# Gated mix of sliding-window attention and ReGLU with its gradients: the last stage in two passes, weight turns moved there, and more attention units turned in pairs by DMA

## The chip, the cores and the metric

The kernel runs on one core of one Trainium2 chip, in one launch. The metric is the device time in microseconds (us), as the median of several runs. Runs of one kernel agree within about 0.2%.

## What is computed

The reference computes an output and, by `jax.vjp`, the gradients of seven inputs. Cut to what matters (S = 2048 tokens, D = 512, F = 1376, 32 heads of 16, window 256, all bf16):

```python
def _A_ref(x, wqkv, wo):                      # sliding-window attention
    q, k, v = split_heads(x @ wqkv)           # 32 heads of 16
    scores = where(0 <= i - j < 256, q @ k.T * 16 ** -0.5, -1e9)
    return merge_heads(softmax(scores) @ v) @ wo

def _B_ref(x, W_gate, W_up, W_down):          # ReGLU
    gate = x @ W_gate
    h = relu(gate) * (x @ W_up)
    return h @ W_down

g = sigmoid((x * gate_w).sum(-1, keepdims=True))
out = g * _A_ref(x, wqkv, wo) + (1 - g) * _B_ref(x, W_gate, W_up, W_down)
# returned: out, and the gradients of x, wqkv, wo, W_gate, W_up, W_down, gate_w
```

## The kernel before

Tokens are handled in 16 tiles of 128. TensorE (PE) multiplies, VectorE (DVE) and ScalarE (ACT) evict and do elementwise work, GpSimd (POOL) masks and does small products, and the SyncE queue (SP) issues nearly all transfers in the order in which its program lists them.

**Stage 1, the feed-forward part** (to about 250 us). For 11 chunks of F and four groups of 512 tokens it computes h, the gradients of gate and up (`dgT`, `duT`), and the gradients of the three feed-forward weights. h, dgT and duT are written to DRAM, transposed to F x S (`hT_d`, `dgT_d`, `duT_d`).

**Stage 2, attention** (to about 721 us). Four head groups c of eight heads, and in each 16 block rows j of 128 queries. A block row meets up to three key blocks: the diagonal one (role "d"), the one before (role "m") and the far one (role "f"), each in two halves of four heads. One such piece is a *unit*: 90 a head group, 360 in all. A unit computes scores (`ST`, L683), their exponent on ACT (L693), a mask on POOL for roles d and f (L695, L698), the gradient of the probabilities (`dPT`, L707), its product on DVE (L712), and row sums (`BA`, L721 and L723). For the key-side gradients (`CD`, L541 and L544) the probabilities must be turned, in `flip`. There are two ways: by DMA, where both halves of a role go in one `dma_start_transpose` of 512 KB on the SP queue (a *pair*, `u.pair`, L740) or one half alone goes in 256 KB (`u.dma`); or on PE, in eight 128x128 transposes (`pt`, L750) and an eviction. Roles d always go in pairs and roles f always on PE. Roles m go in pairs in the first three head groups; in the last one:

```python
u.pair = u.role == "d" or (u.role == "m" and (c < DC - 1 or j in (3, 5, 7, 9)))
u.dma = u.pair or (u.role == "m" and half == 0 and (c < DC - 1 or j < 10))
```

The order of stage 2 is written by hand, unit by unit (`tc.manual_schedule()`): what is due after which unit stands in a queue of events, and background work is inserted by a running credit. The background work is the next group's projections (`project_parts`, L133 and L136), the previous head group's weight gradient (`grad_parts`, 16 pieces of four matmuls, `wps` at L637) and, from the dictionary `plan`, the loads of stage 3's weights. Those of Wqkv, Wg and Wu are turned by DMA out of DRAM, two 128-column chunks at a time (`turns`, L581). Their tiles reuse the slots of the transposed inputs (`x0` to `x3`, `d0` to `d3`) and of the projection weights (`p0` to `p3`) as these come free. `clear` (L584) zeroes on POOL the rows that the last, partial chunk of Wg or Wu leaves unused. At the end of a quarter of the block rows the key-side results are spilled to DRAM (`spill`, L564, into `dqkvo_d`).

**Stage 3, per token tile** (from about 721 us). For each of 16 tiles: `dwo` (4 matmuls, the output weight's gradient), `bps` (11, h x Wdown), `aps` (4, attention output x Wo), `dxps` (22 from dgT x Wg and duT x Wu, L1062, and 12 from the turned dqkv x Wqkv, L1066), then elementwise work and two stores. Loads come for groups of two tiles (`load_group`): h, dgT and duT (704 KB each), grad_out (`go_g`, 256 KB), the attention outputs (`o_g`, two of 128 KB), and a turn of 256 rows of `dqkvo_d` (1 MB, L845). For group 0 that turn is done early, in four parts, during stage 2 (`early_group`, L805), and h and dgT too (`early_f`). Stage 3 is not under the manual schedule. There the framework's scheduler orders each engine's instructions by its own costs, and may set an instruction that the program text has later between those of stage 2, where its buffers allow.

Of the kernel before, what the change touches and what calls it, by code (L numbers as in the profile page):

```python
# [9 lines left out]
ALU = mybir.AluOpType  # L10
# [12 lines left out]
def kernel(  # L23
# [490 lines left out]
    if True:  # L514
# [84 lines left out]
        def loads(name, src, k0, tag):  # L599
            def one(k):  # L600
                if (tag, "t") not in W6:
                    W6[(tag, "t")] = slot(tag)
                load_rows(name, src, k, W6[(tag, "t")][:, k - k0, :])
            return [lambda k=k: one(k) for k in range(k0, min(k0 + 4, FC))]
# [8 lines left out]
        def load_gw():  # L613
# [63 lines left out]
        def front(u):  # L677
# [6 lines left out]
            if not u.own:  # L684
                if u.half == 0:
                    kind = "m" if u.c == DC - 1 and u.j == 12 else u.role
                    tag = f"PP{kind}"
# [107 lines left out]
        def early_group():  # L795
            a = st.tile([P, NT, 4, P], BF, tag="rows_st", name="early")[:].rearrange("p t a n -> p (t a n)")
            n1 = 4 * DC * GT * P
            S2["T0"] = a[:, 0:n1].rearrange("p (c s) -> p c s", c=4 * DC)

            def grads():  # L800
                S2["grads"] = grad_parts(DC - 1, True)

            out = [grads]
            for k in range(4):
                out.append(lambda k=k: nc.sync.dma_start_transpose(out=S2["T0"][:, 4 * k:4 * (k + 1), :],  # L805
                                                                   in_=dqkvo_d[0:GT * P, k * D:(k + 1) * D]))
            return out

# [5 lines left out]
        def early_f(i):  # L814
            flat = wq.tile([P, 2, TPG, NP, P], BF, tag=f"z{i}", name=f"f{i}")[:].rearrange("p w k h q -> p (w k h q)")
            S2[f"f{i}"] = flat[:, 0:FC * GT * P].rearrange("p (c s) -> p c s", c=FC)
            load_f(S2[f"f{i}"], (hT_d, dgT_d)[i], slice(0, GT * P))

        def load_group(g):
            gsl = slice(g * GT * P, (g + 1) * GT * P)  # L820
            if g == 0:
                T_g, hT_g, dgT_g = S2["T0"], S2["f0"], S2["f1"]
                go_g = S2["g6"].tile([P, GT, D], BF, tag="go_g", bufs=1)
            else:
                flat = st.tile([P, NT, 4, P], BF, tag="rows_st", name="gt")[:].rearrange("p t a n -> p (t a n)")
                n1, n2 = 4 * DC * GT * P, (4 * DC + FC) * GT * P
                T_g = flat[:, 0:n1].rearrange("p (c s) -> p c s", c=4 * DC)
                hT_g = flat[:, n1:n2].rearrange("p (c s) -> p c s", c=FC)
                go_g = flat[:, n2:n2 + GT * D].rearrange("p (t d) -> p t d", t=GT)
                dgT_g = S2["g6"].tile([P, FC, GT * P], BF, tag="dgT_g")  # L830
                load_f(hT_g, hT_d, gsl)
            duT_g = S2["g6"].tile([P, FC, GT * P], BF, tag="duT_g")
            o_g = S2["g6"].tile([P, GT, DC, P], BF, tag="o_g")
            nc.sync.dma_start(go_g[:] if g == 0 else go_g, go_d[gsl, :].rearrange("(t p) d -> p t d", p=P))
            if g > 0:
                load_f(dgT_g, dgT_d, gsl)
            if g == 0:
                load_f(duT_g, duT_d, gsl)
            o_v = dqkvo_d[gsl, :].rearrange("(t p) (c a n) -> p t c a n", p=P, c=DC, a=4)
            for tl in range(GT):  # L840
                nc.sync.dma_start(o_g[:, tl, :, :], o_v[:, tl, :, 3, :])
            if g > 0:
                load_f(duT_g, duT_d, gsl)
            if g > 0:
                nc.sync.dma_start_transpose(out=T_g, in_=dqkvo_d[gsl, :])  # L845
            return hT_g, dgT_g, duT_g, T_g, go_g, o_g

        with tc.manual_schedule():
# [11 lines left out]
            early = []  # L860
# [25 lines left out]
            while n <= NU + LAG or ev or cdq or bgq:  # L886
                now = ev.pop(n, [])
                u = units[n] if n < NU else None
                if u is not None:
# [13 lines left out]
                    if u.first and u.j == TPG - 1 and u.c > 0:  # L903
                        bgq += ready
                    front(u)
                    if u.last and gi + 1 == len(groups) and u.j % TPG in (1, 3):
                        ev.setdefault(n + 2, []).append(("dma", lambda i=(u.j % TPG) // 2: early_f(i)))
# [65 lines left out]
                if u is not None and u.c == DC - 1 and not bgq and u.j > 6 and "T0" not in S2:  # L973
                    early = early_group()
# [4 lines left out]
                if early and calm and (u is None or n % 3 == 0 and u.j >= (9 if len(early) > 4 else 13)):  # L979
                    early.pop(0)()  # L980
# [10 lines left out]
            grp_next = load_group(0)  # L991
# [7 lines left out]
    with ExitStack() as p56:  # L999
        x_r5 = x_r  # L1000

        with ExitStack() as p6:
# [7 lines left out]
            dwo_ps = [ps6.tile([P, D], F32, name=f"dwo{c}") for c in range(DC)]  # L1010

            def add_dwo(t, tl, go_g, o_g):
                da_r = t6.tile([P, D], BF, tag="da_r", name="da_r")
                nc.vector.tensor_scalar(da_r[:], go_g[:, tl, :], g_all[:, t:t + 1], None, op0=ALU.mult)
                for c in range(DC):
                    nc.tensor.matmul(dwo_ps[c][:], lhsT=o_g[:, tl, c, :], rhs=da_r[:], start=t == 0, stop=t == NT - 1)
                if t == NT - 1:
                    for c in range(DC):
                        ws = t6.tile([P, D], BF, tag="ws", bufs=5, name="ws")
                        evac(ws[:], dwo_ps[c][:], ("act", "dve")[c % 2])  # L1020
                        nc.sync.dma_start(out_3[c * P:(c + 1) * P, :], ws[:])

            for g in range(NG):
                hT_g, dgT_g, duT_g, T_g, go_g, o_g = grp_next
                if g + 1 < NG:
                    grp_next = load_group(g + 1)
                for tl in range(GT):
# [3 lines left out]
                    if t > 0:  # L1031
                        add_dwo(t, tl, go_g, o_g)
                    bps = ps6r.tile([P, D], F32, tag="bps", bufs=1)
                    for fc in range(FC):
# [102 lines left out]
```

## Time and profile before

| | us |
|---|---|
| median of 3 runs (lowest, highest) | 909.26 (908.79, 910.39) |
| the profiled execution's own time | 911.05 |
| its span, first to last instruction | 909.4 |
| PE busy, share of the span | 895.0, 98% |
| DVE, ACT, POOL busy | 511.8, 441.3, 491.7 |
| SP's transfers (hardware queue 1), share of 16 DMA engines | 86.8% |
| granted TensorE clock | 1.000 |

Terms of the profile: L740 is line 740 of the kernel. "SPq" is the SP queue, whose bars are the issuing of transfers, not their way through the DMA engines. In the timeline a row has the start, the duration, the engine, the line, the operation and the tile written and read. In the chain of waits each row is a piece of the work that ended last, with its start and duration. A matmul's own bar is longer than the distance between matmuls, since they are pipelined; distances are used here.

### The profile page before, as it was taken

The page shows a single profiled execution, that of the slowest core. Times are in us where ns is not written, and L with a number is a line of the kernel's source. Part 1 is how long each engine was busy: PE and PEld are TensorE (multiplying, and loading weights), DVE is VectorE, ACT ScalarE, POOL GpSimd, SP SyncE. Part 2 cuts the span into 40 slices and gives each one's busy share as a digit, 9 for nine tenths or more (in the row PEclk, how much of TensorE's full clock was granted, in tenths as well). Part 3 has the DMA queues.
Part 4 walks back from the last instruction along what each step waited for, and adds up shares of the span by engine and source line. Part 5 has one row for each costly group of instructions (what it writes and reads, how often), then busy time and mean ns, then how long its engine had stood idle before and what let it go on. Part 6 is the DMA issues. An engine that isn't in the chain of part 4 may idle for free.

```text
span 909.4 us, 26127 instructions
## 1 busy us (share of the span) xinstructions
PE 895.0 (98%) x10711; PEld 566.7 (62%) x10711; DVE 511.8 (56%) x952; ACT 441.3 (49%) x778; POOL 491.7 (54%) x937
## 2 busy tenths in 40 slices
PE   9999999999989999999999999999999999999998
PEld 5555656655657777667776677766777644444445
DVE  4433334324468887678886788876787222333223
ACT  6422232222278777667776677766788211100001
POOL 4644545545267778767777567875677312222221
PEclk9999999999999999999999999999999999999999
DMA  9998879999799999999999989999999998777731
GB/s 301 203 194 186 197 179 207 211 207 216 180 143 158 180 188 194 184 175 156 177 185 187 180 161 182 187 182 184 184 185 186 235 269 227 186 181 185 182 86 46
DMA packets 505575, 169.06 MB, mean 186 GB/s; under 512 B 433456, under 2 KB 504336, under 8 KB 505456
## 3 DMA queue, kind: packets, MB, share of 16 engines
q1 hardware_dynamic: 484816, 145.51, 86.8%
q10 hardware_dynamic: 19008, 17.31, 7.2%
q0 software_dynamic: 1632, 4.59, 1.4%
q8 instruction: 83, 1.36, 0.6%
q14 instruction: 36, 0.29, 0.1%
HBM read 32.28 MB, written 36.24 MB: 75 GB/s over the span
## 4 chain that ended last, share of the span: by engine, by line
PE 80%; DMA 5%; DVE 4%; POOL 3%; issue 3%; SPq 2%; ACT 2%; ACTq 0%; POOLq 0%; DVEq 0%
PE dxps L1062 8%; PE ST L683 8%; PE dPT L707 7%; PE pt L750 6%; PE wps L412 5%; PE wps L637 5%; PE dxps L1066 4%; PE CD L541 4%; PE bps L1035 4%; PE BA L721 4%; PE pp L133 4%; PE dps L414 3%; PE ups L363 3%; PE gps L363 2%; PE CD L544 2%
## 5 line engine op out<-in xcount | busy, mean ns | idle before, releaser
L683 PE MATMUL ST<-z,K 128*128 128x512 bf16 x360 | 135.8, 378 | 2.6 <-DVE PPm L712 1.2
L707 PE MATMUL dPT<-z,V 128*128 128x512 bf16 x360 | 136.0, 378 | 1.9 <-DVE Pd L712 0.5
L695 POOL TENSOR_SCALAR_AFFINE_SELECT PPd<-PPd 128x512 bf16<-128x512 bf16 x126 | 80.0, 635 | 86.7 <-ACT PPd L693 86.7
L377 POOL TENSOR_TENSOR hT<-rg,upm 128x512 bf16<-128x512 bf16 x44 | 51.8, 1176 | 116.0 <-DVE upm L375 104.3
L412 PE MATMUL wps<-dgu_r,x_r 128*128 128x256 bf16 (+1 forms) x704 | 103.9, 270 | 1.8 <-DVE wst L74 1.8
L712 DVE TENSOR_TENSOR PPd<-PPd,dPT 128x512 bf16<-128x512 bf16 x126 | 85.4, 678 | 18.3 <-PE dPT L707 9.1
L698 POOL TENSOR_SCALAR_AFFINE_SELECT Pu<-Pu 128x512 bf16<-128x512 bf16 x112 | 71.9, 642 | 31.8 <-ACT Pu L693 30.7
L412 PEld LDWEIGHTS <-x_r 128*128 128x128 bf16 x704 | 68.4, 98 | 33.1 <-issue 2.6
L712 DVE TENSOR_TENSOR Pd<-Pu,dPT 128x512 bf16<-128x512 bf16 x112 | 76.3, 681 | 21.5 <-POOL Pu L698 10.6
L693 ACT ACTIVATE PPd<-ST 128x512 bf16<-128x512 f32 x126 | 76.1, 605 | 22.0 <-PE ST L683 19.7
L712 DVE TENSOR_TENSOR PPm<-PPm,dPT 128x512 bf16<-128x512 bf16 x122 | 81.4, 668 | 7.8 <-PE dPT L707 6.1
L693 ACT ACTIVATE Pu<-ST 128x512 bf16<-128x512 f32 x112 | 67.4, 602 | 34.1 <-PE ST L683 33.6
L693 ACT ACTIVATE PPm<-ST 128x512 bf16<-128x512 f32 x122 | 73.7, 604 | 20.2 <-PE ST L683 19.6
L1042 ACT COPY a_sb<-aps 128x512 f32<-128x512 f32 x16 | 9.4, 586 | 151.4 <-issue 137.7
L375 DVE SCALAR_TENSOR_TENSOR upm<-rg,ups 128x512 bf16<-128x512 bf16 x44 | 30.1, 685 | 82.9 <-ACT rg L369 40.3
L369 ACT ACTIVATE rg<-gps 128x512 bf16<-128x512 f32 x44 | 26.3, 598 | 91.8 <-PE gps L363 44.2
L72 ACT COPY p<-pt 128x1024 bf16<-128x1024 bf16 x67 | 68.5, 1022 | 3.8
L414 PE MATMUL dps<-db_r,h_r 128*128 128x512 bf16 x176 | 66.7, 379 | 0.0
L387 POOL TENSOR_TENSOR dgu<-dh_sb,rg 128x512 bf16<-128x512 bf16 x44 | 56.7, 1289 | 5.3 <-ACT dh_sb L383 5.3
L1048 POOL DMA_DIRECT2D out_dram<-o_sb x16 | 8.7, 542 | 88.8 <-DVE o_sb L1046 82.4
L637 PE MATMUL wps<-rows_st,x_r 128*128 128x384 bf16 x256 | 50.3, 325 | 0.0
L133 PE MATMUL pp<-x,p 128*128 128x512 bf16 x192 | 49.0, 378 | 0.0
(193 smaller groups left out, 2357.5 us busy)
## 6 DMA issues: line engine op xcount, KB each, us to landing
dqkvo_d<-rows_st SPq DMA_DIRECT2D x15, 512.0 KB, 4.0
hT_d<-hT ACTq DMA_DIRECT2D x44, 128.0 KB, 2.5
dgT_d<-dgu ACTq DMA_DIRECT2D x44, 128.0 KB, 3.0
duT_d<-dgu ACTq DMA_DIRECT2D x44, 128.0 KB, 2.9
duT_g<-duT_d SPq DMA_DIRECT2D x8, 640.0 KB, 5.2
gt<-hT_d SPq DMA_DIRECT2D x7, 640.0 KB, 5.8
dgT_g<-dgT_d SPq DMA_DIRECT2D x7, 640.0 KB, 5.0
out_dram<-wst SPq DMA_DIRECT2D x20, 128.0 KB, 2.7
```

What stands on the lines that cost most here:

```text
L72: nc.scalar.copy(out, in_)
L133: nc.tensor.matmul(pp[:], lhsT=w_p[c][:, cd, which * P:(which + 1) * P], rhs=x_T[tg][:, cd, :], start=(cd == 0), stop=(cd == DC - 1))
L412: nc.tensor.matmul(acc["w"][:, c, 0:2 * nw], lhsT=x_r[:, t, c * P:(c + 1) * P], rhs=k.dgu_r[:, :, i, s0:P], start=(go_ and c % 2 == 0), st ...
L414: nc.tensor.matmul(acc["d"][:], lhsT=k.h_r[:, i, :], rhs=db_r[:, t, :], start=go_, stop=no_)
L637: nc.tensor.matmul(wps[:], lhsT=x_r[:, t, part * P:(part + 1) * P], rhs=sts[c][:, t, 0:3, :], start=first and t == t0, stop=last and t == ...
L683: nc.tensor.matmul(ST[:], lhsT=KTt[:, ksl], rhs=z[:, 0, :, jl, :], start=True, stop=True)
L693: nc.scalar.activation(u.Pu[:], ST[:], ACT.Exp)
L695: nc.gpsimd.affine_select(out=u.Pu[:], in_=u.Pu[:], compare_op=ALU.is_ge, fill=0.0, base=0, pattern=[[0, HH], [1, P]], channel_multiplier=-1)
L698: nc.gpsimd.affine_select(out=u.Pu[:], in_=u.Pu[:], compare_op=ALU.is_ge, fill=0.0, base=-1, pattern=[[0, HH], [-1, P]], channel_multiplier=1)
L707: nc.tensor.matmul(u.dPT[:], lhsT=VTt[:, ksl], rhs=z[:, 1, :, jl, :], start=True, stop=True)
L712: nc.vector.tensor_tensor(out=u.Pd[:], in0=u.Pu[:], in1=u.dPT[:], op=ALU.mult)
L1062: nc.tensor.matmul(to, lhsT=src[:, fc, lsl], rhs=W6[(wt, fc)][:, cols], start=(fc == 0 and wt == "Wg"), stop=False)
```

## The change

1. Stage 3 becomes two passes over the tiles. Pass one has `bps` and `dwo`; the product with Wdown is copied by ACT into a buffer `b_all` in SBUF. Pass two has `aps` and `dxps` and reads `b_all`. The loads split in two: `load_a` (h, grad_out, attention outputs) and `load_b` (turned dqkvo, dgT, duT, grad_out again). `load_b` turns 1 MB for every group; the early turn in four parts is gone.
2. The turns of Wu and of the last chunks of Wg leave `plan` for a list `W_rest`, taken from in pass one, two items a group. Wdown is loaded in three whole transfers and a rest in place of eleven.
3. In the last head group role m goes in pairs for all block rows but the last two; single halves by DMA are gone.
4. The third head group's gradient pieces are released in four portions (at block rows 3, 6, 10, 12) in place of one.

The core of the diff:

```diff
         plan = {2: [load_gw], 5: turns("wqkv", A_wqkv, 0, 4, "p0"), 7: turns("wqkv", A_wqkv, 4, 8, "p1"),
                 11: turns("wqkv", A_wqkv, 8, 12, "p2"),
                 12: turns("Wg", B_W_gate, 0, 4, "x0") + turns("Wg", B_W_gate, 4, 8, "d0"),
-                13: turns("Wg", B_W_gate, 8, 12, "x1") + turns("Wu", B_W_up, 0, 4, "d1") + [lambda: clear("Wg")],
-                14: turns("Wu", B_W_up, 4, 8, "x2") + turns("Wu", B_W_up, 8, 12, "d2"),
-                15: loads("Wd", B_W_down, 0, "x3") + [lambda: clear("Wu")] + loads("Wd", B_W_down, 4, "d3") + loads("Wd", B_W_down, 8, "p3") + [load_wo]}
+                15: loads("Wd", B_W_down, 0, "x3") + loads("Wd", B_W_down, 4, "d3") + loads("Wd", B_W_down, 8, "p3")}
+        W_rest = (turns("Wg", B_W_gate, 8, 12, "x1") + [lambda: clear("Wg")] + turns("Wu", B_W_up, 0, 4, "d1") + turns("Wu", B_W_up, 4, 8, "x2")
+                  + turns("Wu", B_W_up, 8, 12, "d2") + [lambda: clear("Wu")])
...
-                        u.pair = u.role == "d" or (u.role == "m" and (c < DC - 1 or j in (3, 5, 7, 9)))
+                        u.pair = u.role == "d" or (u.role == "m" and (c < DC - 1 or j < NT - 2))
                         u.own = u.role == "f"
-                        u.dma = u.pair or (u.role == "m" and half == 0 and (c < DC - 1 or j < 10))
+                        u.dma = u.pair
...
+        def load_a(g):
+            if g > 1:
+                load_h(g)
+            S2[f"go{g}"] = load_go(g)
+            o_v = dqkvo_d[tokens(g), :].rearrange("(t p) (c a n) -> p t c a n", p=P, c=DC, a=4)
             for tl in range(GT):
...
+                o_t = pjA.tile([P, DC, P], BF, tag=("K0", "K1", "V0", "V1")[t % 4], name="o_t")
+                nc.sync.dma_start(o_t[:], o_v[:, tl, :, 3, :])
+                S2[f"o{t}"] = o_t
+
+        def load_b(g):
+            if g % 2 == 0:
+                S2["T"] = st.tile([P, NT, 4, P], BF, tag="rows_st", name="turned")[:].rearrange("p t a n -> p (t a n)")
+            n1 = 4 * DC * GT * P
+            T_g = S2["T"][:, g % 2 * n1:(g % 2 + 1) * n1].rearrange("p (c s) -> p c s", c=4 * DC)
+            nc.sync.dma_start_transpose(out=T_g, in_=dqkvo_d[tokens(g), :])
...
-                    if u.first and u.j == TPG - 1 and u.c > 0:
-                        bgq += ready
+                    if u.first and u.c > 0 and u.j in ((3, 6, 10, 12) if u.c == DC - 1 else (3,)):
+                        k = NT // 4 if u.c == DC - 1 else NT
+                        bgq += ready[:k]
+                        del ready[:k]
...
-            grp_next = load_group(0)
+            while late:
+                late.pop(0)()
+            load_a(0)
+            for _ in range(2):
+                W_rest.pop(0)()
+            load_a(1)
...
+            for t in range(NT):
+                g, tl = t // GT, t % GT
+                if tl == 0:
+                    if 0 < g < NG - 1:
+                        load_a(g + 1)
+                    for _ in range(2):
+                        if W_rest:
+                            W_rest.pop(0)()
+                    if g == NG - 2:
+                        load_wo()
+                    if g == NG - 1:
+                        grp_next = load_b(0)
...
+                nc.vector.tensor_scalar(da_r[:], S2[f"go{g}"][:, tl, :], g_all[:, t:t + 1], None, op0=ALU.mult)
+                bps = ps6r.tile([P, D], F32, tag=f"r{t % 3}", name="bps")
+                for fc in range(FC):
+                    nc.tensor.matmul(bps[:], lhsT=S2[f"h{g}"][:, fc, lsl], rhs=W6[("Wd", fc)],
+                                     start=(fc == 0), stop=(fc == FC - 1))
+                nc.scalar.copy(b_all[:, t, :], bps[:])
                 for c in range(DC):
...
+                    nc.tensor.matmul(dwo_ps[c][:], lhsT=S2[f"o{t}"][:, c, :], rhs=da_r[:], start=t == 0, stop=t == NT - 1)
```

In the order in which the built programs' instructions stand on each engine, stage 2 before has 104 more PE transposes than after. On SP, after, the six turns of Wu and the first two whole turns of `dqkvo_d` stand among the last head group's pairs; the two turns of Wg's end stand behind its last pair. On POOL, after, the zeroing of Wu's last rows stands before the mask of unit d of block row 4 (second half) of the last head group.

More of the change, by code (lines that the diff above doesn't have):

```diff
@@ L599, in loads, with whole @@
         def loads(name, src, k0, tag):
[L600 to L604, printed above, removed]
+            k1 = min(k0 + 4, nfull)
+            def whole():
+                W6[(tag, "t")] = slot(tag)
+                for k in range(k0, k1):
+                    W6[(name, k)] = W6[(tag, "t")][:, k - k0, :]
+                nc.sync.dma_start(W6[(tag, "t")][:, 0:k1 - k0, :], src[k0 * P:k1 * P, :].rearrange("(c p) d -> p c d", p=P))
+            return [whole] + [lambda k=k: load_rows(name, src, k, W6[(tag, "t")][:, k - k0, :]) for k in range(k1, min(k0 + 4, FC))]
         def load_wo():
@@ L793 @@
         NG = NT // GT
[L795 to L807, printed above, removed]
         def load_f(dst, src_d, gsl):
@@ L1009 @@
             pending_dgw = None
-            dwo_ps = [ps6.tile([P, D], F32, name=f"dwo{c}") for c in range(DC)]
-            def add_dwo(t, tl, go_g, o_g):
-                da_r = t6.tile([P, D], BF, tag="da_r", name="da_r")
-                nc.vector.tensor_scalar(da_r[:], go_g[:, tl, :], g_all[:, t:t + 1], None, op0=ALU.mult)
-                for c in range(DC):
[L1016 to L1021, printed above, removed]
+            dwo_ps = [ps6.tile([P, D], F32, tag=f"w{c}", name=f"dwo{c}") for c in range(DC)]
@@ L1030 @@
                     lsl = slice(tl * P, (tl + 1) * P)
[L1031 to L1034, printed above, removed]
-                        nc.tensor.matmul(bps[:], lhsT=hT_g[:, fc, lsl], rhs=W6[("Wd", fc)],
-                                         start=(fc == 0), stop=(fc == FC - 1))
-                    aps = ps6r.tile([P, D], F32, tag="aps", bufs=1)
+                    aps = ps6r.tile([P, D], F32, tag=f"r{t % 2}", name="aps")
                     for c in range(DC):
```

81 lines of the change are left out of this document (33 added, 48 removed).

## The prediction

> **What bounds the kernel now.** I read the page first (slices, chain of waits), then the chain in order of time for the last 300 us, the timelines of SP, PE and POOL through the attention stage, groups by tile, and the order in which both programs' instructions stand on each engine. The page's chain by engine:
>
> ```profile
> PE 80%; DMA 5%; DVE 4%; POOL 3%; issue 3%; SPq 2%; ACT 2%; ACTq 0%; POOLq 0%; DVEq 0%
> ```
>
> PE holds the end nearly everywhere. In the last stage the chain in order of time is the same five rows for each of 16 token tiles, without a gap:
>
> ```profile
> 744.01 0.86 PE dwo L1016 x4
> 744.87 2.37 PE bps L1035 x11
> 747.25 0.86 PE aps L1039 x4
> 748.11 4.75 PE dxps L1062 x22
> 752.94 2.61 PE dxps L1066 x12
> ```
>
> 2.37/11 is 0.216 us a matmul; a tile has 53, 11.5 us. Next the SP queue, where a bar begins when the instruction's waits are over. First a stretch of the third head group, which the change leaves alone:
>
> ```profile
> 540.76 1.96 SPq L740 DMA_TRANSPOSE p2m<-PPm  x1
> 542.83 3.81 SPq L740 DMA_TRANSPOSE p2d<-PPd  x1
> ...
> 557.17 3.28 SPq L740 DMA_TRANSPOSE p2m<-PPm  x1
> 560.61 2.77 SPq L740 DMA_TRANSPOSE p2d<-PPd  x1
> ```
>
> Eight turned pairs (512 KB each) stand end to end here in 22.6 us: 2.8 us each, or 185 GB/s. In the last head group SP goes on like this without a pause. I added its bars from 591.7 (after the spill at 591.0) to the end of the last pair,
>
> ```profile
> 703.69 6.14 SPq L740 DMA_TRANSPOSE p2d<-PPd  x2
> ```
>
> that is 709.8: 20 pairs 61.6 us (3.08 each), 5 half pairs 6.2, 14 weight turns 20.9 (1.49), 3 turns of rows 4.6, 4 "early" turns 5.2, 19 plain transfers 12.6 (0.66): 111 of 118.1 us. The queue is as full as PE. Only slack keeps it off the chain: the last pair landed near 712.5 (5.6 us after issue is the median) and PE reads it 5.2 us later:
>
> ```profile
> 717.73 0.18 PE L541 MATMUL CD<-rq,p2d 128*128 128x32 bf16 x1
> ...
> 718.14 2.90 PE L637 MATMUL wps<-rows_st,x_r 128*128 128x384 bf16 x16
> 720.87 0.81 PE L1035 MATMUL bps<-x,f 128*128 128x512 bf16 x3
> ```
>
> **The change part by part: PE.** The two passes run 15 and 38 matmuls a tile, 53 as before: 0. Thirteen units are no longer turned on PE (the second halves of block rows 1, 2, 4, 6, 8; both halves of 10 to 13). The chain shows such a unit as 0.46 us for its 8 transposes: 13 x 0.46 = -6.0 us, all on the chain. Their evictions (1.02 us on ACT or 0.69 on DVE) go too, but stand beside PE: 0. The third group's gradient pieces (0.65 us each) only spread out. The kernel's tail keeps its matmuls; PE has no gap over 0.1 us before its last half tile (900.8), so freeing the buffer there brings 0 to -0.3; I take 0.
>
> The Trainium skill's TensorE: Matmul & The Clock Gate, Part 4: PE-mode transpose, gives about 275 ns for one transpose inside a kernel; by that the 104 would save an estimated 28.6 us. The trace does not agree: they follow each other at 0.46/8 = 58 ns.
>
> **SP in the last head group.** The built order tells what the diff doesn't: the turns of Wu stand outside the hand-written schedule, and the scheduler puts all six of them back into the attention stage, with two whole 1 MB turns of dqkvo for the second pass; only the two of Wg's end stay behind. From the same spill to the last pair SP now has 29 pairs, 12 weight turns, 3 rows, 2 whole turns, 17 plain transfers. At 2.8, 1.49, 1.55, 5.8 and 0.66 us, with 1.9 for gaps: 81.2 + 17.9 + 4.6 + 11.6 + 11.2 + 1.9 = 128.4 us, against 118.1. (A whole turn lies between 5.2, four early ones at 1.31, and 6.3, the median of its own row in the last stage; I take the middle, as the queue has few other loads there.) That is +10.3, less the slack of 5.2: +5.1 at the stage's end. With pairs at 3.08, this stretch's own mean, +13; at 2.6, -1, which PE's own pace replaces at -6.0.
>
> **A new wait on POOL.** The zeroing of Wu's last rows (L584, 0.5 us) waits for the turn that fills them, and stands on POOL just before the select of the diagonal unit of block row 4, second half. Everything later queues behind it: the selects, so DVE's products, so PE's row sums. That select ran here:
>
> ```profile
> 618.62 0.64 POOL L695 TENSOR_SCALAR_AFFINE_SELECT PPd<-PPd 128x512 bf16<-128x512 bf16 x1 [1.81 <-ACT PPd L693]
> ```
>
> After the change POOL gets there about 3.5 us sooner (two turned units, 0.9, and four gradient pieces put off, 2.6): 615.1. SP reaches the end of that weight turn after 7 pairs, 8 weight turns, one of rows and two plain transfers: 591.7 + 19.6 + 11.9 + 1.55 + 1.3 = 626.1; its issue began at 624.6, and such turns land thus:
>
> ```profile
> DMA to landing us min/median/max: 3.6/5.0/6.1
> ```
>
> 629.6, and the memset ends at 630.1: POOL is 15.0 us late. PE works about two units (2.5 us) ahead of a select, so 12.5 us come off it. -6.0 + 12.5 = +6.5. Ends: pairs at their shortest bar (1.77) and the quickest landing leave about 6, pairs at 3.08 with the slowest 18.
>
> The two delays run beside each other: while POOL waits, SP works off its queue, so the later one decides, plus some idling of SP when PE then feeds it late. I take +9 (ends -6 and +16). To stay at zero cost the turn would have to land by about 617.6, 12 us before my estimate.
>
> **Pass one.** It has 15 x 0.216 = 3.24 us a tile, 6.5 us for a group's h (704 KB), go and o (256 KB each), on two h buffers: h of group g+1 may be issued only when group g-1 is through. From the stage's start T: SP's list puts a whole turn (6.3 us, the loaded median) straight before h of group 5. It follows an o that waits for tile 6 (T+22.7), so h is issued at about T+29.7 instead of T+25, lands 6.2 later (5.8 median and its first issue) at T+35.9, and is wanted at T+32.4: 3.5 late. The same before group 7: 2.7. Bytes: six h, ten go, 16 o, four dgT or duT, two whole turns and small ones, 4.2 + 2.6 + 2.0 + 2.8 + 2.1 + 0.8 = 14.5 MB in 57 us (with 5 us of head start), 254 GB/s, while the stage's best 10 us windows moved 281 to 286, so there is little to catch up with. I take +5; 0 if the turns are quick and h needs only its issue and 5 us, 10 if the early groups slip too. The 52 us of tiles hide the rest.
>
> **Pass two** has 38 matmuls, 16.6 us a group, for 2.7 MB of loads and 9 us of SP time: 0, as the last stage before carried 3.65 MB in 23 us. The whole turns come two groups ahead.
>
> **Sum.** +9 + 5 = +14 us on the profiled span of 909.4, so 923.4; the time around the span (911.05 - 909.4 = 1.65) stays. The profiled run is 1.8 above the median of the three, 909.26, so the median goes to 923.
>
> **The rivals.**
> - *Cheap turns* (faster). If a pair holds SP only for its shortest bar, 1.77 us, SP's total is 98 us and never binds; if in addition the weight turn lands before POOL gets there, all of PE's 6.0 us stay and pass one is fed: 909.3 - 6.0 = 903.5. It decides when that turn lands by 617.6. For: single bars of 1.8 to 2.1 exist. Against: each is followed by one of 2.8 to 3.8, the sum of two is 5.2 to 6.1. Chance 0.10.
>  The Trainium skill's DMA: Bandwidth & Descriptors, Latency and other measured facts, has a DMA transpose at 261 GB/s; by that a pair would be an estimated 2.0 us and the queue would not bind. The trace gives 185 GB/s end to end.
> - *Only the POOL wait or only pass one costs something*, the other is hidden: -6 + 6 to 12.5, or 0 + 5: 909 to 915. For: SP's slack of 5.2 and 6 us of head start for pass one. Chance 0.23, a fifth of it within 0.2%.
> - *The forecast*: the full last head group and a few late h: 915 to 935. Chance 0.57.
> - *Pass one bound by transfers throughout*: its 14.5 MB at the mean 186 GB/s of the page take 78 us instead of 57, +21 in place of +5: 939. For: the turns from DRAM are slow. Against: 281 and 286 GB/s in windows of this stage. Chance 0.10.
>
> That the change doesn't do what it says is in the forecast already: were the Wu turns really moved, SP would have 8.9 us less and POOL no wait, which leads to the first rival.
>
> **How the numbers follow.** The likeliest case gives 923. The range is 907 to 937: it leaves out most of the first rival and the last one. 0.2% is 1.8 us, about what a measurement of this kernel tells from none. Faster 0.12 (the first rival and a bit of the second), same 0.05, slower 0.83.
>
> **What would show it.** In the profile after: 104 fewer transposes on the line that turns units on PE, SP without a pause from 592 to past 720; POOL idle for 10 us or more at L584 near 615 to 630, PE idle beside it; the first bps near 730 instead of 720.87; gaps in PE before tiles 10 and 14 of pass one. The prediction is wrong if PE has no gap near 620 and the first bps starts before 718, or if pass two, which I hold for gapless, stalls.

## The result, and the profile after

The changed kernel takes 935.33 us (median of 6 runs, 933.81 to 938.13), the kernel before 910.32 in the same comparison (6 runs, 908.79 to 910.55): ratio 1.028, 95% interval 1.0265 to 1.0300. The forecast was 923, its range 907 to 937: the time lies inside the range, but the loss, 25.0 us, is nearly twice the forecast's 13.7 (923 against 909.26). The profiled execution has a span of 934.8 us, 25.4 more than before, and it takes 1.8 us more than its span.

Stages by the first ST of the last head group, the first `bps` and the first `aps` in the trace:

| | before | after | difference |
|---|---|---|---|
| up to the last head group (same work) | 585.0 | 582.9 | -2.1 |
| last head group to first `bps` | 135.9 | 148.9 | +13.0 |
| pass one (before: 15 of 53 matmuls a tile, 51.7) | 51.7 | 66.6 | +14.9 |
| the rest | 136.8 | 136.4 | -0.4 |

The first row is no effect of the change: over all traces of this study the last head group begins between 582.5 and 585.9. So stages are compared by their lengths. From the page of the changed kernel, PE and granted clock in 40 slices of 23.4 us, and the chain by engine:

```profile
PE   8999999999999999999999999969997888999998
...
PEclk9999999999999999999999999988999989999999
...
PE 65%; issue 11%; POOL 8%; DMA 6%; SPq 3%; DVE 3%; ACT 3%; POOLq 0%; ACTq 0%; DVEq 0%
```

Two places show, slice 27 (the last head group) and slices 31 to 34 (its end and pass one), and the clock beside them (27, 28 and 33); before, PE and clock were at 9 in all of these. The chain's larger shares of POOL and "issue" come mostly from stage 1, where it now runs through POOL's products; that stage is no longer than before.

**The last head group.** POOL's timeline (the bracket is the idle time before the row and what ended it):

```profile
617.80 0.40 POOL L781 TENSOR_TENSOR rows_st<-BAs,rinv 128x128 bf16<-128x128 f32 x1
629.17 0.51 POOL L584 MEMSET d<- 32x512 bf16 x1 [10.97 <-DMA d<-in_B_W_up_dram]
629.65 0.62 POOL L701 TENSOR_SCALAR_AFFINE_SELECT Pu<-Pu 128x512 bf16<-128x512 bf16 x1
```

This is the wait that the forecast named, and it ended where the forecast put it (629.7, forecast 630.1). PE has a hole of 8.6 us beside it (622.4 to 631.0). Stretches of 2 us; columns: length, PE busy (instructions), granted clock, DMA share, GB/s:

```profile
622.00:624.00 2.00, 0.45 (x8) 1.00 1.26 124
624.00:626.00 2.00, 0.00 (x0) 0.98 1.01 295
626.00:628.00 2.00, 0.00 (x0) 0.50 0.89 169
...
634.00:636.00 2.00, 2.00 (x14) 0.50 1.23 256
636.00:638.00 2.00, 2.00 (x32) 0.96 0.72 120
```

The clock falls to half 3.5 us after PE stops and stays there for 5 us after PE has begun again. Yet this hole is not what the stage pays for, as the runs below show. SP went on through it, and at the stage's end it still had this to do:

```profile
692.28 2.27 SPq L743 DMA_TRANSPOSE p2d<-PPd  x1
694.64 5.36 SPq L832 DMA_TRANSPOSE turned<-dqkvo_d  x1
...
703.60 1.85 SPq L743 DMA_TRANSPOSE p2d<-PPd  x1
705.50 5.90 SPq L832 DMA_TRANSPOSE turned<-dqkvo_d  x1
...
717.88 7.63 SPq L743 DMA_TRANSPOSE p2d<-PPd  x2
```

The last pair ends at 725.5 (before 709.8). Two whole turns stand between pairs, and PE waits for the pairs behind them: before `CD` and `ST` it has gaps of 1.0, 2.4, 1.4 and 1.6 us from 698 on. The first `bps` follows 6.3 us after the last pair, where it was 11.0.

**Pass one.** PE at the first and longest gap, and what SP did before it issued that h:

```profile
744.87 1.03 PE L1029 MATMUL dwo<-da_r,o_t 128*128 128x512 bf16 x4
752.24 1.89 PE L1025 MATMUL bps<-x,h 128*128 128x512 bf16 x4 [6.35 <-DMA h<-hT_d]
```

```profile
730.46 4.05 SPq L581 DMA_TRANSPOSE x<-in_B_W_gate_dram  x2
...
737.18 4.98 SPq L633 DMA_DIRECT2D out_dram<-ws  x4
...
743.87 0.43 SPq L799 DMA_DIRECT2D duT_g<-duT_d  x1
...
746.03 0.38 SPq L799 DMA_DIRECT2D h<-hT_d  x1
```

h of group 2 goes into the buffer that tile 1 gave up at about 739. It is issued at 746, behind two weight turns, four stores of gradients and the first loads of pass two, and PE waits for it. Gaps of 2.3 and 1.3 us follow before tiles 10 and 14, and 0.8 us before the first `dwo`: 10.8 us in all. The first four `bps` matmuls after the long gap take 1.89 us, elsewhere 1.03: the clock is at half again. Tile 4's eleven take 4.05 instead of 2.37, tile 10's about 1.5 us too many: 3.2 us more. Gaps and clock make 14.0 of the 14.9 us.

**Pass two** has no gap over 0.25 us. The chain in order of time, start and duration:

```profile
831.72 0.86 PE aps L1045 x4
832.59 4.75 PE dxps L1068 x22
837.41 2.61 PE dxps L1072 x12
```

### The profile page after: what moved, and what is told of

Read it like the earlier page. It is cut to its first block, busy times and chain, and to the rows that moved or that the text cites. A ratio compares the mean times of both kernels' runs of the same rounds, so it can differ in the third digit from the quotient of the medians.

```text
span 934.8 us, 25877 instructions
## 1 busy us (share of the span) xinstructions
PE 890.2 (95%) x10506; PEld 562.0 (60%) x10607; DVE 508.0 (54%) x946; ACT 445.2 (48%) x787; POOL 497.1 (53%) x937
## 4 chain that ended last, share of the span: by engine, by line
PE 65%; issue 11%; POOL 8%; DMA 6%; SPq 3%; DVE 3%; ACT 3%; POOLq 0%; ACTq 0%; DVEq 0%
PE dxps L1068 8%; PE ST L687 8%; PE dPT L710 7%; PE pt L753 5%; PE wps L641 5%; PE dxps L1072 4%; POOL dgu L387 4%; PE CD L541 4%; PE BA L724 4%; PE pp L133 4%; PE bps L1025 3%; PE CD L544 3%; POOL hT L377 2%; PE BA L726 2%; DMA h<-hT_d 2%
## 5 line engine op out<-in xcount | busy, mean ns | idle before, releaser
L687 PE MATMUL ST<-z,K 128*128 128x512 bf16 x360 | 136.5, 380 | 14.4 <-DVE Pd L715 8.6
L710 PE MATMUL dPT<-z,V 128*128 128x512 bf16 x360 | 136.4, 379 | 1.3 <-ACT PPd L696 0.5
L715 DVE TENSOR_TENSOR PPd<-PPd,dPT 128x512 bf16<-128x512 bf16 x128 | 86.9, 679 | 21.4 <-PE dPT L710 12.1
L1057 POOL TENSOR_TENSOR amb<-amb,go_g 128x512 f32<-128x512 f32 x16 | 24.6, 1540 | 73.8 <-DMA out_dram<-ws 62.9
L72 ACT COPY p<-pt 128x1024 bf16<-128x1024 bf16 x59 | 60.1, 1019 | 4.6 <-PE pt L753 0.5
L414 PE MATMUL dps<-db_r,h_r 128*128 128x512 bf16 x159 | 60.3, 379 | 0.0
L1079 POOL DMA_DIRECT2D out_dram<-dx_sb x15 | 8.1, 541 | 74.4 <-DVE dx_sb L1077 64.5
```

The costliest lines, as they stand in the source:

```text
L414: nc.tensor.matmul(acc["d"][:], lhsT=k.h_r[:, i, :], rhs=db_r[:, t, :], start=go_, stop=no_)
L687: nc.tensor.matmul(ST[:], lhsT=KTt[:, ksl], rhs=z[:, 0, :, jl, :], start=True, stop=True)
L710: nc.tensor.matmul(u.dPT[:], lhsT=VTt[:, ksl], rhs=z[:, 1, :, jl, :], start=True, stop=True)
L715: nc.vector.tensor_tensor(out=u.Pd[:], in0=u.Pu[:], in1=u.dPT[:], op=ALU.mult)
```

## The experiments

Lengths of stages are taken from each run's trace as in the table above ("attention" is the last head group to the first `bps`). The ratio is to the kernel before, with its 95% interval. The trace is of one execution: for e7 (916.4 us) and e10 (915.4) it is the longest of eight (910.2 to 916.4) and of ten (911.7 to 915.4), 4.1 and 2.3 us above the median, so their stage lengths are less typical than the others'.

| run | attention | pass one | median us | ratio |
|---|---|---|---|---|
| the change | 148.9 | 66.6 | 935.3 | 1.028 (1.0265 to 1.0300) |
| e1_clear_late | 148.1 | 64.0 | 933.1 | 1.0255 (1.0237 to 1.0273) |
| e2_pass_one_in_order | 138.0 | 53.5 | 915.6 | 1.0060 (1.0045 to 1.0075) |
| e3_pairs_as_before | 142.6 | 58.9 | 923.3 | 1.0146 (1.0127 to 1.0165) |
| e4_turns_in_the_plan | 151.4 | 58.2 | 931.5 | 1.0238 (1.0221 to 1.0255) |
| e5_pairs_alone | 144.4 | - | 918.6 | 1.0099 (1.0084 to 1.0114) |
| e6_passes_alone | 140.6 | 57.7 | 920.6 | 1.0115 (1.0098 to 1.0133) |
| e7_order_by_hand | 133.8 | 59.6 | 912.3 | 1.0030 (1.0014 to 1.0045) |
| e8_order_by_hand_wg | 129.4 | 64.1 | 916.6 | 1.0080 (1.0063 to 1.0097) |
| e9_h_on_act | 148.0 | 62.7 | 932.3 | 1.0241 (1.0210 to 1.0271) |
| e10_by_hand_h_on_act | 133.0 | 57.5 | 913.1 | 1.0030 (1.0017 to 1.0042) |
| e11_by_hand_wg_h_on_act | 129.5 | 59.3 | 910.6 | 1.0007 (0.9995 to 1.0020) |
| e12_fewer_bytes | 146.5 | 65.5 | 934.4 | 1.0270 (1.0257 to 1.0283) |
| e13_by_hand_late_turn | 129.4 | 51.8 | 907.2 | 0.9969 (0.9956 to 0.9982) |
| e14_by_hand_wg_back | 133.3 | 51.8 | 909.0 | 0.9990 (0.9980 to 0.9999) |
| e15_by_hand_wo_early | 130.6 | 52.6 | 905.3 | 0.9947 (0.9934 to 0.9959) |
| e16_by_hand_h_on_sp | 129.4 | 56.5 | 909.3 | 0.9988 (0.9977 to 0.9998) |
| e17_by_hand_units_on_pe | 134.9 | 51.9 | 910.1 | 0.9998 (0.9988 to 1.0007) |

### POOL's wait or SP's queue

The zeroing of Wu's rows held back:

```diff
-                  + turns("Wu", B_W_up, 8, 12, "d2") + [lambda: clear("Wu")])
+                  + turns("Wu", B_W_up, 8, 12, "d2") + [lambda: clear_late("Wu")])   # writes b - b of tile 5
```

> The change, with one edit: the zeroing of Wu's last rows is made to need the result of token tile 5 of pass one (it writes b - b there), so it can no longer stand in POOL's queue in the last head group; the turns stay where they are. In the changed kernel POOL idles 10.97 us before that memset and PE has a hole of 8 us (622.4 to 631.0). Theory QUEUE (SP sets the end of the attention stage: its bars from the spill at 589.2 to the last turned pair at 725.5 fill 131.4 of 135.8 us, so the hole on PE is covered by it): the hole goes, the first bps moves by 0 to -2 from 732, the time stays at 933 to 935. Rival POOL (the hole is lost for good, and what SP shows later follows from it): the first bps comes 8 us sooner, near 724, and the time is 925 to 928, with 2 us of it from the TensorE clock that stays at 1.00 around 626 to 636.

The hole at 622 is gone and the stage is only 0.8 us shorter. The waits of PE in this run, from the last head group on (engine, line, what it waited for: us, times, longest):

```profile
PE CD L541 <- DMA p2m<-PPm: 9.5, 5, 4.4
PE ST L692 <- ACT PPd L701: 2.5, 2, 1.6
```

PE, let through, runs into the next turned pair: a gap of 4.4 us at 640.6, and the same tail of gaps. QUEUE holds: the first `bps` comes 0.5 us sooner (731.3), the time, 933.1, is the one it gave.

The choice of units of before:

```diff
-  u.pair = u.role == "d" or (u.role == "m" and (c < DC - 1 or j < NT - 2))
+  u.pair = u.role == "d" or (u.role == "m" and (c < DC - 1 or j in (3, 5, 7, 9)))
-  u.dma = u.pair
+  u.dma = u.pair or (u.role == "m" and half == 0 and (c < DC - 1 or j < 10))
```

> The change, with the choice of turned units of the kernel before: thirteen units of the last head group are turned on PE again. SP has 20 pairs and 5 halves instead of 29 pairs, about 20 us less; PE has 6 us more. Theory QUEUE: SP ends some 16 us sooner than PE needs, so the stage is PE's again: first bps near 719 + what of the POOL wait is left on PE (about 4, since the Wu turn comes up 5 us sooner on SP) = 721 to 724, time 924 to 927. Rival POOL: as the hole is the cost and the pairs were free, turning on PE again adds 6 us less the 4 of the shorter hole: first bps 732 to 734, time 935 to 938.

PE's waits in this run, from the last head group to the end of pass one:

```profile
PE ST L687 <- DVE Pd L716: 6.4, 1, 6.4
PE bps L1026 <- DMA h<-hT_d: 4.6, 4, 2.3
```

Attention 6.3 us shorter although PE has 6 us more to do. The only gap of more than 0.6 us left on PE in this stage is POOL's wait, 6.4 us at 623: with SP relieved, that wait does cost. It is more than the 4 us that were expected, so the first `bps` comes at 725.5 and not by 724; the time, 923.3, is just under the range given.

The turns back in the plan:

```diff
+                13: turns("Wg", ..., 8, 12, "x1") + turns("Wu", ..., 0, 4, "d1") + [lambda: clear("Wg")],
+                14: turns("Wu", ..., 4, 8, "x2") + turns("Wu", ..., 8, 12, "d2"),
+                15: loads("Wd", ..., 0, "x3") + [lambda: clear("Wu")] + ...      # W_rest = []
```

> The change, with the eight turns of Wg's end and Wu and the two zeroings put back into the hand-written plan of the last head group, where the kernel before has them; pairs and the two passes stay changed. SP has two weight turns more before the last pair (3 us), POOL's memset comes later and after its turn. Theory QUEUE: the hole on PE goes, yet the first bps is 2 to 4 us later than 732 (734 to 736), and pass one, free of the 4 us of turns at its head, loses 2 to 4 us less: time 933 to 937. Rival POOL: without the hole the first bps is near 724 to 726, time 924 to 928.

Attention is 2.5 us longer, as QUEUE said, pass one 8.4 us shorter, which is more than said, so the time, 931.5, is under its range. The expectation that POOL's wait goes failed: Wdown's first rows are now one list item and no longer four, so the zeroing comes up earlier in the plan and POOL waits 10.7 us for its turn there.

The kernel before with the new choice of units only (e3's diff, reversed):

> The kernel before, with the change's choice of turned units only (thirteen more units of the last head group are turned by transfers; one pass, weight turns in the plan as before). QUEUE: SP's list between the spill and the last pair grows by nine pairs less five halves, 9 x 2.85 - 6.2 = 19.5 us, from 118.2 to about 137; of the 11.1 us that lay between the last pair and the first bps some 6.4 must stay (so in the changed kernel), so the first bps moves from 720.9 to about 735 and the time is 921 to 926. Rival PE (a queue that was full already takes more, since pairs get shorter when they are packed): the 6 us of PE come off, 902 to 906.

Attention grows by 8.5 us, in QUEUE's direction and 60% of its size; the time, 918.6, is 2.4 us under its range. The 29 pairs took 81.6 us, 2.81 each, where 20 had 3.08 each before: SP's stretch grew by 13.3 us (118.2 to 131.5) and not by 19.5. By the Trainium skill's DMA: Bandwidth & Descriptors, Latency and other measured facts (261 GB/s for a transpose by DMA, measured there with a non-contiguous middle dimension), a pair would be an estimated 2.0 us and this run no slower; the trace has 2.81 us for 512 KB, 187 GB/s.

### Leaving the order of the text

```diff
-            for t in range(NT):
-                g, tl = t // GT, t % GT
+            with tc.manual_schedule():
+                for t in range(NT):
+                    g, tl = t // GT, t % GT
```

> The change, with one edit: pass one of the last stage stands in a hand-scheduled block, so its instructions stay in the order in which they are written; Wu's six turns, the loads of wo and the first whole turn of dqkvo then really lie in pass one, and only the second whole turn is still pulled ahead. Theory QUEUE: SP's list from the spill to the last pair loses 9.8 + 5.6 + 2.9 = 18.3 us, so the first bps comes 16 to 19 us sooner, near 714, the pace that PE sets; POOL has no long idle before a memset. In pass one theory ORDER (h of a group is late because of what stands ahead of it on SP) has at most 3 us of gaps instead of 11, theory BANDWIDTH (14.5 MB in 52 us are too many) the same 11 to 14 as before. The first whole turn and dgT, duT of pass two are issued only two tiles ahead there, so 3 to 8 us of gap stand before the first aps. Time 908 to 915 by QUEUE and ORDER, 918 to 925 by QUEUE and BANDWIDTH, over 925 if QUEUE is wrong.

PE's waits, first of the changed kernel (580 to 800), then of this run (583 to 780):

```profile
PE bps L1025 <- DMA h<-hT_d: 10.0, 3, 6.3
PE ST L687 <- DVE Pd L715: 8.6, 1, 8.6
PE CD L541 <- DMA p2m<-PPm: 4.5, 3, 2.4
```

```profile
PE CD L541 <- DMA p2m<-PPm: 4.3, 3, 2.4
PE dxps L1069 <- DMA dgT_g<-dgT_d: 1.3, 1, 1.3
PE bps L1026 <- DMA h<-hT_d: 1.2, 1, 1.2
```

The largest single step: 19.8 us of the 25 come back (935.3 to 915.6), 0.6 us above the range that QUEUE and ORDER gave together. Five of Wu's six turns and its zeroing are now in pass one (the zeroing runs at 751.4, with nobody waiting; one turn stays at the head of the last head group, at 590.7, here and in the runs by hand below). SP's stretch up to the last pair shrinks from 135.7 to 120.8 us, and pass one has one gap, of 1.2 us. Attention, 138.0, is still 2.1 longer than before: one whole turn remains in it, and PE waits 4.3 us for pairs. What is gone from PE's waits there is POOL's; but e1, without that wait, gained 0.8 us, as PE then waited 9.5 us for pairs. Here the list of SP is shorter too.

### Pass one: order or bytes

Only the two passes, units and plan as before (the diffs of e3 and e4 together):

> The change, with both the choice of turned units and the plan of weight turns as in the kernel before: only the two passes of the last stage are left. QUEUE: SP has before's pairs and turns, 5.2 us of early turns replaced by 11.2 us of whole turns, fewer single loads; it stays within before's slack, so the first bps comes at 719 to 722. Pass one, with no weight turns at its head, takes 58 to 59 us instead of 52 as in the run with the turns in the plan: time 915 to 919. If the pass-one losses are due to bytes alone they are the same 14 us as in the change: 922 to 926.

The first `bps` comes at 724.6, later than said, since POOL waits for the zeroing here too (5.7 us), and the run is 1.6 us above its range for it. Pass one is 57.7, about as said.

h of groups 2 to 7 on ACT's queue:

```diff
-            load_f(S2[f"h{g}"], hT_d, tokens(g))
+            load_f(S2[f"h{g}"], hT_d, tokens(g), nc.scalar if g > 1 else nc.sync)
```

> The change, with one edit: the six loads of h for groups 2 to 7 of pass one are issued from ACT's queue instead of SP's, so nothing but the eviction of the tile before stands ahead of them; bytes, buffers and what the last head group does are unchanged (first bps 731 to 733 from a start of that head group at 583). ORDER (what stands ahead of h on SP makes the 11 us of gaps and 3.2 us of half clock): pass one 52 to 55 us instead of 66.6, time 921 to 924. BANDWIDTH (the transfers of the stage cannot carry more, whoever issues them): pass one 62 to 67 us, time 931 to 936. Between the two, 56 to 61 us, both have a share.

Only 3.9 us came, as BANDWIDTH said. ACT's timeline shows why the first gap stayed:

```profile
736.83 0.59 ACT L1027 COPY b_all<-bps 128x512 f32<-128x512 f32 x1 [2.60 <-PE bps L1025]
741.43 0.41 ACTq L799 DMA_DIRECT2D h<-hT_d  x1
```

The buffer was free at 736.8, and the issue still waited until 741.4. At that moment a store of a weight gradient that SP had issued at 737.3 (`out_dram<-ws`) landed: in the trace all transfers of SP and ACT share eight semaphores, and the wait before h's first issue ended with the landing of the earlier transfer on its own semaphore. In this program a queue of its own does not free h from the transfers ahead.

Fewer bytes in about the same order (the loads of dgT and duT for groups 0 and 1 cut to one block of ten):

```diff
+            load_f(dgT_g, dgT_d, tokens(g), 1 if g < 2 else nfull)
+            load_f(duT_g, duT_d, tokens(g), 1 if g < 2 else nfull)
```

> The change, but the loads of dgT and duT for groups 0 and 1 of pass two fetch one of their ten row blocks (64 KB instead of 640 KB each), and the two groups' matmuls use that block for all ten: part of the gradient's input is left out, PE's work and the number of loads stay, 2.3 MB less are moved while pass one runs. BANDWIDTH (the stage moves 229 to 241 GB/s in every run so far, whatever the order): 2.3 MB / 0.237 = 9.7 us less, pass one 56 to 58 us instead of 66.6, time 924 to 927. ORDER (h waits behind other issues, however small they are): pass one 63 to 67 us, time 931 to 936.

The 56 to 58 us that BANDWIDTH gave did not come: pass one took 65.5 us with 12.9 MB at 197 GB/s. But the order did not stay the same. In this build a whole turn also stands straight before h of group 2, and the gap there is 9.2 us instead of 6.4, so the run does not show what fewer bytes alone are worth:

```profile
746.45 4.39 SPq L832 DMA_TRANSPOSE turned<-dqkvo_d  x1
750.94 0.52 SPq L799 DMA_DIRECT2D h<-hT_d  x1
```

### The order by hand

On top of e2: `load_t(g)` is split from `load_b(g)` and placed in the text, Wg's last turns come after the second group's loads.

```diff
+                        if g == 4:
+                            load_t(0)
+                        if g == 5:
+                            load_t(1)
```

> Pass one in order, as in the earlier run, and more: both whole turns for groups 0 and 1 of pass two are written into pass one (behind the loads for tiles 10 and 12), Wg's last turns behind the second group's loads. None of it stands in the last head group now. QUEUE: SP's list there is 5.5 us shorter than with one whole turn in it (115 instead of 120.8), so most of the four gaps of 5.2 us and the 3.4 us at half clock that were left in the attention stage go: first bps 714 to 718. Pass one carries about 2 MB more than in the earlier run: ORDER has at most 3 us of gaps in it, BANDWIDTH 6 or more. Time 905 to 910 by QUEUE and ORDER, 911 to 916 by BANDWIDTH.

> As the run before it, and the first four turns of Wg leave the last head group for pass one too (5.9 us of SP's time there). QUEUE: the list is some 109 us, PE sets the pace in the whole attention stage: first bps 712 to 714. Pass one has ten more loads on SP in its second half and 1 MB more: by ORDER 0 to 4 us of gaps, by BANDWIDTH 10 or more. Time 903 to 908 or over 912.

The attention stage does as QUEUE says in both: 133.8, and 129.4 with no gap on PE. Pass one takes it back, 59.6 and 64.1, and the times are those that BANDWIDTH gave. But in both h of the next group also stands behind whole turns of 5 us again, and pass one carried more: 14.4 and 15.1 MB, against 12.1 in e2. With h on ACT's queue:

> The order by hand with both whole turns in pass one (912.3 us, pass one 59.6), and h of groups 2 to 7 on ACT's queue. ORDER: pass one 52 to 54 us, time 904 to 907, faster than before. BANDWIDTH: pass one 58 to 61, time 911 to 914.

> The same with four turns of Wg in pass one too (916.6 us, pass one 64.1, attention stage without a gap), and h on ACT's queue. ORDER: pass one 52 to 55 us, and with the attention stage 129.4 us from the last head group's first ST to the first bps the time is 902 to 906. BANDWIDTH: pass one 62 to 65, time 914 to 918.

2.1 and 4.8 us better in pass one, and still 57.5 and 59.3; the medians show it only in the second (912.3 and 913.1; 916.6 and 910.6). ORDER, if it means the issuing queue alone, fails here; BANDWIDTH holds in the first, and the second lies between the two. The next step moves the whole turns themselves out of h's way (one behind the loads for tile 14, one in pass two, which is put in order by hand too):

```diff
-                        if g == 4:
-                            load_t(0)
-                        if g == 5:
-                            load_t(1)
+                        if g == 6:
+                            load_t(0)
```

> The whole last stage in the written order, all of Wg and Wu turned in pass one, h of groups 2 to 7 on ACT's queue, one whole turn of dqkvo in pass one (behind the loads for tile 14) and the second at the start of pass two. Attention stage as in the run with Wg moved (129.4 us from the last head group's first ST to the first bps). BANDWIDTH: pass one has 1 MB less than the 13.9 MB it had with both turns there, 12.9 / 0.237 = 54 to 56 us, pass two gapless: time 904 to 909. ORDER: the same or 1 to 2 us less, as h is on a queue of its own already. Slower than 910 only if pass two now waits for its first turns.

> The same, but the four turns of Wg stay in the last head group as in the change (5.9 us of SP there). QUEUE: attention stage 133 to 134 us as in the first run by hand; BANDWIDTH: 1 MB less in pass one, at or near PE's pace, 52 to 54 us: time 906 to 911. If QUEUE and BANDWIDTH both hold, this and the run before it differ by less than 3 us: what one stage gains the other loses.

Pass one is at PE's pace, 51.8 us, in both, below the 54 to 56 that bytes alone would have made of the first. It moved 12.5 MB at 242 GB/s there, nearly what the run with fewer bytes carried in 65.5 us. So the place of the transfers counts. That it alone decides is not shown: with a whole turn less, pass one also carries 1.6 to 1.9 MB less than in e10 and e11 (14.4 and 14.1 MB), and at the 238 to 250 GB/s of those two runs 12.5 MB take 50 to 53 us, no more than PE's own pace.

Part of the first run's gain moves on: its rest takes 140.3 us, 136.8 in e11. PE waits 2.1 us for dgT before the first `dxps`, and its clock is at half for 3.4 us.

Then wo's loads back into the last head group, and two controls:

```diff
-                        if g == NG - 2:
-                            load_wo()
+   15: loads("Wd", ...) + ... + [load_wo]}
```

> The 907 us version with one edit: the four loads of wo (2 us of SP's time, straight before dgT and duT of pass two's first group) go back into the last head group, whose queue has some 6 us of room there. The gap of 2.1 us before the first dxps of pass two and most of its 3.4 us at half clock go, the attention stage keeps its 129.4 us: time 903 to 906 by ORDER. If the loads were late for bytes and not for their place: 906 to 908.

> The same version with h back on SP's queue, in the written order (h first in its group, two weight turns behind). ORDER on the queue: h of a group waits for up to two turns of the group before, 3 to 5 us, with about 3 us of room: pass one 54 to 57 us, time 906 to 911. If only the place of the whole turns had mattered: pass one 52, no change to the run beside it.

> The same version with the thirteen units back on PE. If the saving on PE is real once SP has room, this run is 5 to 7 us slower than the one beside it (908 to 911); if turning by transfers costs what it saves, within 2 us of it.

905.25 us for the first, 0.5% faster than the kernel before. Its stretches (attention, pass one, pass two; length, PE, PEld, DVE, ACT, POOL busy, clock, DMA share, GB/s):

```profile
582.50:713.10 130.60, 128.06 (x2244) 91.53 (x2251) 89.68 (x166) 86.79 (x155) 91.51 (x213) 1.00 1.15 198
713.10:765.70 52.60, 52.03 (x237) 23.18 (x240) 5.57 (x17) 9.92 (x18) 1.03 (x2) 1.00 1.14 237
765.70:903.40 137.70, 132.75 (x695) 64.16 (x706) 51.96 (x115) 20.20 (x36) 36.03 (x47) 1.00 0.79 186
```

PE is busy for all but 2.5 and 0.6 us of the first two, and the clock is whole. The controls: h back on SP costs 4.1 us (pass one 56.5 instead of 52.6), the thirteen units back on PE cost 4.8 us (attention 134.9 instead of 130.6). The first control is the clean test of ORDER: only the queue of h differs, pass one carries 12.8 and 12.5 MB, and PE, which waits 0.3 us for h in the one, waits 4.2 us in the other:

```profile
PE bps L1032 <- DMA h<-hT_d: 4.2, 3, 1.8
```

## Why the prediction was right and wrong

**Right: direction, places and signs.** Slower, and inside the range, just above the 915 to 935 of the likeliest case. 104 fewer transposes (those that read `PPm`: 136 before, 32 after), SP full from 590 to past 720, POOL idle 11 us before its memset, the first `bps` near 730 (731.8), gaps before tiles 10 and 14, a gapless pass two.

**PE, -6.0: right, but not had.** Where SP has room the stage is 129.4 against 135.9, and units back on PE cost 4.8 us. In the changed kernel the saving turns into waiting for pairs.

**POOL's wait: right in place, right in being covered.** Forecast: SP gets to the turn's issue at 624.6, it lands at 629.6. Trace: 625.6 (the second turn of the two that begin at 623.8) and 629.1. PE's hole was 8.6 us instead of 12.5. The forecast said that the later of the two delays decides; that is what holding back the zeroing showed (0.8 us of the stage).

**SP's list: the term that was mis-sized in the attention stage.** Taken +9 for the stage, measured +13.0. The listed prices held, within 1.6 us each: 29 pairs 82.8 us (81.2 forecast), 12 weight turns 18.7 (17.9), two whole turns 11.3 (11.6). Missing were above all 4.0 us of pauses between instructions and 1.7 us of plain transfers; SP took 135.7 us where the forecast had 128.4. The pauses were there to be seen: the forecast's own list of the kernel before fills 111 of 118.1 us, so 7 us are pauses, and for the changed kernel it allowed 1.9 (measured 5.9). The slack of 5.2 us was right (4.7 used). SP's measured stretch, 17.5 us longer, less this slack gives +12.8. The forecast took the later of its two delays, +5.1 on SP and +6.5 on POOL, and added some 2.5 us for SP's idling; the trace shows no such idling (SP's pauses were 6.9 us before), but a longer list.

**Pass one, +5: the step that failed.** Measured +14.9. The two late loads that were worked out, before tiles 10 and 14, cost 2.3 and 1.3 us (forecast 3.5 and 2.7). Missed was the first, before tile 4, of 6.35 us: "the early groups slip too" stood there as an upper end of 10 and not as the expected case, and no time was worked out for them. But the built order had Wg's turns, four stores and pass two's loads in front of that h: its buffer was free at about 739, and it was issued at 746. Smaller, 0.8 us stood before the first `dwo`. Not in the forecast at all: the clock, 3.2 us in pass one. The forecast's argument by rate (254 GB/s wanted, 281 to 286 seen) was no help: the runs with gaps moved 197 to 250, and those at PE's pace 237 to 242.

**The rivals.** *Cheap turns* did not come: a pair costs 2.8 us when the queue binds. *Only the POOL wait or only pass one* did not come either: POOL's wait was hidden, and both stages cost. *Pass one bound by transfers throughout* gave a time nearer to the measured one, but not by what happened: its 186 GB/s throughout did not come (229), and pass one cost 14.9 us and not 21. That the change does not do what it says was counted as part of the forecast; it is the larger part, since with pass one in the order of the text 19.8 us come back.

**What stays open.** How pass one's loss divides between the place of h on the queue, the sum of bytes, and the shared semaphores was not separated. The place alone is worth 4.1 us at nearly equal bytes (e15 and e16). Up to 13.5 MB the sum of bytes alone does not explain a loss: in the kernel before and in e5 the first 51.7 us of the last stage carry 13.1 and 13.5 MB and PE has no gap, while e12 took 65.5 us for 12.9. But no run brought 13.7 MB or more through pass one in under 57.5 us, and the changed kernel carried 15.2 in 66.6 (229 GB/s); a longer pass one also collects more of pass two's loads, so this alone shows no cause. Why e10 and e11 stay 6 to 8 us above PE's pace is open.

## What to carry to other kernels

When work is moved to an idle place, look in the built order whether it stayed there: a scheduler that may reorder pulled transfers ahead, onto the fullest queue. Price a queue as the sum of all its bars, small ones and pauses too, before the prices of single waits; a wait beside a full queue costs little until the queue has room (0.8 us in e1, 6.4 in e3). In a stage that lives on double-buffered loads, work out when the first of them can be issued, not only the later ones, and let nothing long stand between two of them on the queue. Putting the loads on another queue repaired only part of that here.

## What the runs showed of the hardware

- PE's granted clock fell to half 3.5 us after PE stopped (the hole of 8.6 us), and the first matmuls after the gap of 6.4 us ran at half speed (eleven in 4.05 us instead of 2.37). The changed kernel's dips last 3.4, 6.8 and 10.2 us. The Trainium skill's TensorE: Matmul & The Clock Gate, Part 1, has a free-running window of about 3.4 us of idleness before the fall and of work before the return. Lengths and halving agree. But shorter gaps were enough for a dip of 3.4 us here, one of 2.3 us (773.5 to 775.8) and in e10 one of 1.5 us (before 687.3), while one of 2.6 us in e6 had none.
- A turned pair's bar on SP is no fixed price. The mean in the last head group is 2.75 to 2.86 us in the six runs whose stretch of SP up to the last pair is 131 to 136 us long (2.85 in the change, 2.81 in e5), 2.96 to 3.09 in those with a shorter stretch (before, 3.08 for its 20 pairs; e15, 89.7 us for 29), and 2.7 in e17, whose queue pauses for 35 of 115 us. What sets it was not tested.
